# An RWKV attention stage rebuilt on 64-token chunks of two batch rows, ahead of a routed expert layer

## The chip, the cores and the metric

The kernel runs on one core of one Trainium2 chip, as one launch. The metric is the device time of that launch in microseconds. Its engines are TensorE (PE, with its weight loads shown apart as PEld), VectorE (DVE), ScalarE (ACT), GpSimd (POOL) and SyncE (SP, which here only issues DMAs). All tensors are fp32 except the one-hot matrices of the routing.

## The reference: what is computed

Two blocks stand one after the other. The first is a linear attention with a delta-rule state, for 4 batch rows, 8 heads, 768 tokens and a head dimension of 40:

```python
for t in range(S):
    y[:, :, t] = einsum('bhd,bhde->bhe', r_t, state)
    Sa = einsum('bhde,bhe->bhd', state, a_t)
    state = state * w_t[:, :, None, :] - einsum('bhd,bhe->bhde', Sa, b_t) + einsum('bhd,bhe->bhde', v_t, k_t)
```

The second takes the 3072 rows of 320 values that come out and runs a top-1 routed expert layer on them:

```python
logits = x @ w_gate                       # 8 experts
expert_idx = argmax(logits, axis=1)       # and the softmax weight of that expert: gate_w
y = relu(x_e @ w1[e]) @ w2[e]             # rows of expert e, F = 1024
out = gate_w[:, None] * y
```

## The kernel before

The token recurrence is turned into matrix products over chunks of 128 tokens of one batch row. A unit is one chunk of one row with all 8 heads; there are 24 units, and a batch row's six chunks follow one another through its state. Two heads lie above each other on the partitions (`rows(par)`, 40 of each 64), and four such pairs lie beside each other (`p`).

`prepare` (L154) forms the running product of the decays (four scans and a reciprocal on DVE), scales A, K and B by it, and turns V, K, B and the decay into token-major form by PE transposes. `systems` (L195) builds four products of 128x128 per head under a triangular mask: GT, NT, N and AT, from operands of 40 rows. Inside a chunk each token's update depends on the tokens before it, so a unit triangular system (1 - N) has to be solved. The kernel squares N five times (`product`, L187, once for N and once for its transpose, each a group of four 128x128 matmuls and an ACT copy out of PSUM) and `attend` (L219) applies the powers in turn to the right-hand side: eight steps of `apply` (L226), each four matmuls of 128x128 weights on 40 columns and one DVE addition (L252, L261), for each of the two halves. Then come the transposed solution (L265), the product ZT under its mask, the output (L279 to L293), the new state (L300, L306) and its transpose (L323). `route` (L328) computes the gate logits of the unit (L336, L340) and its softmax weight, scales the rows by it and stores them to a DRAM tensor `x_rows`.

The units are software-pipelined in the program text (`prepare` and `systems` of the next unit stand before `attend` of this one). The order on each engine is set by the framework's scheduler, which sorts the instructions by a modelled time; no order is written out by hand.

After the last unit the routing (L387 to L485) counts the tokens of each expert and builds gather and scatter indices, all on a few DVE instructions, two matmuls and one-hot products. Then eight experts follow in fixed groups of four tiles of 128 rows: an indirect gather from `x_rows` on the POOL queue, transposes, `layer1` (L514), `layer2` (L527), a copy out (L532) and an indirect scatter (L533). Expert weights come on SP's queue, the first two pairs after attention. A loop over overflow tiles ends the kernel (L562).

## Time and profile before

| what | value |
|---|---|
| median of 3 runs | 2147.67 us (2145.57 to 2150.49) |
| the profiled execution | 2146.03 us, of which the span from first to last instruction is 2144.2 us |
| PE busy | 2009.8 us, 12916 matmul records |
| DVE, ACT, POOL busy | 511.5, 417.3, 151.1 us |
| mean granted TensorE clock | 0.756 of full |
| DMA moved | 59.58 MB |

"Busy" is the time in which an engine had at least one instruction under way. PE's matmuls overlap, and a record's duration contains its way through the array: in a row such as "1.05 us x16" the spacing of the starts is what an instruction costs, not the mean duration. Each fp32 matmul appears as two records, each with its own weight load. The granted clock is 1.00 at 2.4 GHz and 0.50 at 1.2 GHz; a value between is a mean over a stretch that had both.

### The profile page before, as it was taken

To read this page: it belongs to the slowest core of one execution; us is meant where nothing else is said; L and a number is where in the kernel's file an instruction comes from. 1 tells how busy PE (TensorE), PEld (TensorE's weight loads), DVE (VectorE), ACT (ScalarE), POOL (GpSimd) and SP (SyncE) were. 2 spreads that over 40 slices of the span, in tenths; PEclk is the share of its full clock that TensorE was granted. 3 is DMA by queue.
4 is the path that set the end of the run, shared out by engine and by line. 5 is a ranking of instruction groups with operands and counts; after the bars stand their busy time and mean duration, and the time that the engine had idled before them with its cause. 6 is when DMAs were issued, how large, how long until landed. Compare 5 with 4: busy or idle time off the path is not lost.

```text
span 2144.2 us, 29192 instructions
## 1 busy us (share of the span) xinstructions
PE 2009.8 (94%) x12916; PEld 1751.6 (82%) x12916; DVE 511.5 (24%) x1157; ACT 417.3 (19%) x849; POOL 151.1 (7%) x185
## 2 busy tenths in 40 slices
PE   5999999999999999999999999999999876999998
PEld 5899999999998999999999989989898872544454
DVE  3313322232233222222321332232221114111110
ACT  1322122211221222122212212212222100000010
POOL 4000000000000000000000000000000003211011
PEclk9987668756766786678667657866777657999999
DMA  2000000000000000000000000000000005332210
GB/s 56 19 5 23 22 22 19 4 22 19 4 22 22 20 4 22 22 12 12 22 22 1 22 22 20 4 22 22 1 22 4 2 5 149 113 97 71 78 46 12
DMA packets 20560, 59.58 MB, mean 28 GB/s; under 512 B 2893, under 2 KB 14159, under 8 KB 18512
## 3 DMA queue, kind: packets, MB, share of 16 engines
q1 hardware_dynamic: 16992, 48.50, 7.9%
q0 software_dynamic: 3072, 9.18, 1.4%
q8 instruction: 102, 1.67, 0.3%
q14 instruction: 26, 0.21, 0.0%
q10 hardware_dynamic: 368, 0.01, 0.0%
HBM read 49.82 MB, written 9.18 MB: 28 GB/s over the span
## 4 chain that ended last, share of the span: by engine, by line
PE 75%; issue 13%; DVE 4%; POOL 2%; DMA 0%; ACT 0%; POOLq 0%; DVEq 0%; ACTq 0%
PE ps_q L228 20%; PE ps_NT L190 11%; PE ps_N L190 8%; PE ps_y L289 4%; PE ps_y L285 4%; PE ps_r L241 4%; PE ps_nat L169 4%; PE ps_r L235 3%; PE ps_y L279 2%; PE ps_ZT L179 2%; PE ps_GT L179 2%; PE ps_AT L179 1%; POOL out_dram L533 1%; PE ps_N L179 1%; DVE X L252 1%
## 5 line engine op out<-in xcount | busy, mean ns | idle before, releaser
L228 PE MATMUL ps_q<-X,NT 128*128 128x40 f32 x2304 | 352.8, 308 | 36.2 <-DVE X L252 36.2
L228 PEld LDWEIGHTS ps_q<-X,NT 128*128 128x128 f32 x2304 | 334.6, 223 | 48.2 <-DVE X L252 47.3
L190 PE MATMUL ps_NT<-NT,N 128*128 128x128 f32 x1920 | 286.5, 297 | 3.9 <-DVE N L183 2.7
L190 PEld LDWEIGHTS ps_NT<-NT,N 128*128 128x128 f32 x1920 | 244.6, 201 | 12.1 <-DVE N L183 5.1
L192 ACT COPY NT<-ps_NT 128x512 f32<-128x512 f32 x240 | 140.6, 586 | 424.9 <-PE ps_NT L190 424.9
L190 PE MATMUL ps_N<-N,NT 128*128 128x128 f32 x1536 | 212.1, 283 | 0.0
L190 PEld LDWEIGHTS ps_N<-N,NT 128*128 128x128 f32 x1536 | 197.2, 201 | 0.0
L514 PE MATMUL hp<-xgT,w 128*128 128x512 f32 (+1 forms) x384 | 191.4, 628 | 0.0
L252 DVE TENSOR_TENSOR X<-ps_q,X 128x160 f32<-128x160 f32 x240 | 77.9, 325 | 461.0 <-PE ps_q L228 461.0
L514 PEld LDWEIGHTS hp<-xgT,w 128*128 128x128 f32 (+1 forms) x384 | 63.2, 189 | 122.9 <-issue 121.7
L228 PE MATMUL ps_q<-Z,NT 128*128 128x40 f32 x768 | 140.1, 345 | 21.4 <-DVE Z L261 21.4
L228 PEld LDWEIGHTS ps_q<-Z,NT 128*128 128x128 f32 x768 | 132.2, 260 | 28.7 <-DVE Z L261 28.0
L527 PE MATMUL zp<-w,h_sb 128*128 128x320 f32 x512 | 145.0, 433 | 0.0
L192 ACT COPY N<-ps_N 128x512 f32<-128x512 f32 x192 | 112.5, 586 | 75.5 <-PE ps_N L190 75.5
L289 PE MATMUL ps_y<-natB,ZT 128*128 128x40 f32 x384 | 116.1, 415 | 9.4 <-DVE ZT L183 7.9
L527 PEld LDWEIGHTS zp<-w,h_sb 128*128 128x128 f32 x512 | 94.5, 191 | 34.5 <-issue 0.8
L285 PE MATMUL ps_y<-natK,AT 128*128 128x40 f32 x384 | 115.6, 414 | 0.0
L289 PEld LDWEIGHTS ps_y<-natB,ZT 128*128 128x128 f32 x384 | 100.9, 330 | 13.5 <-DVE ZT L183 13.5
L285 PEld LDWEIGHTS ps_y<-natK,AT 128*128 128x128 f32 x384 | 100.6, 329 | 1.6
L158 POOL MEMSET PT<- 128x4 f32 x24 | 2.5, 105 | 1322.8 <-PE ps_xT L336 1010.0
L169 PE MATMUL ps_nat<-ident,in 128*128 128x128 f32 x288 | 71.6, 417 | 24.7 <-DMA in<-in_packed_dram 16.7
L261 DVE TENSOR_TENSOR Z<-ps_q,X 128x160 f32<-128x160 f32 x96 | 31.2, 325 | 225.1 <-PE ps_q L228 225.1
(150 smaller groups left out, 1950.2 us busy)
## 6 DMA issues: line engine op xcount, KB each, us to landing
in<-in_packed_dram SPq DMA_DIRECT2D x48, 480.0 KB
w<-in_moe_w_dram SPq DMA_DIRECT2D x8, 1280.0 KB
w<-in_moe_w_dram SPq DMA_DIRECT2D x8, 1024.0 KB
x_rows<-xs SPq DMA_DIRECT2D x24, 160.0 KB
w<-in_moe_w_dram SPq DMA_DIRECT2D x8, 256.0 KB
xg<-x_rows,g_idx POOLq DMA_INDIRECT x32
out_dram<-zo,s_idx POOLq DMA_INDIRECT x32
wg_sb<-in_moe_w_gate_dram ACTq DMA_DIRECT2D x2, 4.0 KB
```

What stands on the lines that cost most here:

```text
L169: nc.tensor.transpose(ps[:, p, :], src[:, p, :], ident[:])
L179: nc.tensor.matmul(pss[par][:, p, :], lhsT=lhs(par, p), rhs=rhs(par, p), start=True, stop=True)
L190: nc.tensor.matmul(ps[:, p, :], lhsT=lhs[:, p, :], rhs=rhs[:, p, :], start=True, stop=True)
L192: nc.scalar.copy(t[:], ps[:])
L228: nc.tensor.matmul(q[:, p, :], lhsT=m[:, p, :], rhs=x[:, p, :], start=True, stop=True)
L235: nc.tensor.matmul(qs[par][:, p, :], lhsT=I[rows(par), A, p, :], rhs=ST[rows(par), p, :], start=(p == 0), stop=False, skip_group_check=True,)
L241: nc.tensor.matmul(qs[par][:, p, :], lhsT=d["GT"][par][:, p, :], rhs=nV[:, p, par, :D], start=(c == 0 and p == 0), stop=True, skip_group_c ...
L252: nc.vector.tensor_tensor(Xn[:], q[:], X[:], op=ALU.add)
L285: nc.tensor.matmul(qs[par][:, p, :], lhsT=d["AT"][par][:, p, :], rhs=nK[:, p, par, :D], start=(c == 0 and p == 0), stop=False, skip_group_ ...
L289: nc.tensor.matmul(qs[par][:, p, :], lhsT=ZT[par][:, p, :], rhs=nB[:, p, par, :D], start=False, stop=True, skip_group_check=True,)
L514: nc.tensor.matmul(hp[:, :cols], lhsT=g["w"][0][:dsz, db, fb * 128 : (fb + 1) * 128], rhs=g["xT"][:dsz, db, :cols], start=(db == 0), stop= ...
L527: nc.tensor.matmul(zp[:], lhsT=g["h"][:, fb, j * 128 : (j + 1) * 128], rhs=g["w"][1][:, fb, :], start=(fb == 0), stop=(fb == FB - 1),)
```

## The change

A unit is now 64 tokens of two batch rows: `(c, s)` with twelve chunks c and two pairs of rows s. Its sixteen (row, head) systems are `HD`, eight of them side by side (`g`) and two above each other (`par`). Every matmul of the attention works on a 64x64 tile of the array (40 or 64 rows, 64 or 40 columns), or on a 32x32 tile inside the inverse. `eh(par)` is one half of the partitions, `dh(par)` the other: products from `eh` to `eh` lie on the diagonal of the array, those from `eh` to `dh` or back off it. `turns` takes two lists of matmuls and issues two of each in turn.

The triangular system is no longer applied power by power. `invert` forms the inverse of each 64x64 system: both diagonal 32x32 blocks are inverted by four squarings (`inv_sq`) and products (`inv_tt`), with transposes on DVE, and the block below the diagonal is put together from them (`inv_w`, `inv_f`). `solve` then applies it in one product, once for the solution and once for its transpose. The two units of a pair go through each step one after the other.

`manual_schedule` fixes PE's order as the program writes it; the other engines stay with the scheduler. In one iteration PE works on the pair c (right-hand side, solution, state, output, logits) and on the products of the pair c + 1, with the inverse of c + 1 between the two `emit` calls. Loads for c + 2 are issued in iteration c, in pieces of 64 tokens. `emit` forms the token-major rows and their logits in one product with an identity beside the gate weights. The rows are stored unscaled; the softmax weights are computed once for all tokens at the beginning of the routing, written as an extra column of `x_rows`, and come back with the gathered rows, where `layer2` multiplies by them in the copy at L532. The functions not shown (`natural`, `zgram`, `turned`, `y_state`, `y_rest`) are lists of sixteen matmuls of the same kinds, `y_rest` of thirty-two, followed by one copy or one product with a mask.

```diff
--- before.py
+++ after.py
@@ -127,242 +121,488 @@
+        G = 2 * NP
+        T2 = 64
+        NS = S // T2
+        NB2 = B // 2
+        HD = [(g, par) for g in range(G) for par in range(2)]
+        def eh(par, n=D):
+            return slice(par * 64, par * 64 + n)
+        def dh(par, n=D):
+            return slice((1 - par) * 64, (1 - par) * 64 + n)
+        def qd(par, i):
+            q = 2 * (1 - par) + i
+            return slice(q * 32, q * 32 + 32)
+        kab_r = [[ring.tile([128, 2, 3, NP, T2], F32, name=f"kab{s}_{i}") for i in range(3)] for s in range(NB2)]
+        wp_r = [[ring.tile([128, G, T2 + 1], F32, name=f"wp{s}_{i}") for i in range(2)] for s in range(NB2)]
...
+                for lo in (32, 96):
+                    nc.gpsimd.memset(t[lo : lo + 32], 1.0)
+                nc.gpsimd.memset(t[:, :, 0:1], 0.0)
+        first = ring.tile([128, G, T2 + 1], F32, name="first")
+        nc.gpsimd.memset(first[:], 0.0)
+        nc.gpsimd.memset(first[:, :, 0:1], 1.0)
...
+        def turns(*lists):
+            lists = [list(l) for l in lists if l]
+            while any(lists):
+                for l in lists:
+                    for _ in range(2):
+                        if l:
+                            l.pop(0)()
...
+                for par in range(2):
+                    nc.sync.dma_start(
+                        d["wp"][eh(par), b2 * NP : b2 * NP + NP, 1:], packed[b, ch, par, :, W, :, o : o + T2],
+                    )
+                for par in range(2):
+                    nc.sync.dma_start(d["kab"][eh(par), b2], packed[b, ch, par, :, K : B_ + 1, :, o : o + T2])
...
+        def decay(u):
+            c, s = u
+            d = units[u]
+            PT = d["PT"] = sb.tile([128, G, T2 + 1], F32, name=f"PT{s}", bufs=3)
+            nc.vector.tensor_tensor_scan(
+                PT[:].rearrange("q g t -> q (g t)"), d["wp"][:].rearrange("q g t -> q (g t)"),
+                first[:].rearrange("q g t -> q (g t)"), 0.0, op0=ALU.mult, op1=ALU.add,
+            )
+            wi = sb.tile([128, 2, NP, T2], F32, name="wi")
+            P4 = PT[:].rearrange("q (b p) t -> q b p t", b=2)
+            for h in range(2):
+                nc.vector.reciprocal(wi[:, h], P4[:, h, :, 1:])
+            k = d["kab"]
+            for n, m in ((0, wi[:]), (1, P4[:, :, :, :T2]), (2, wi[:])):
+                nc.gpsimd.tensor_tensor(k[:, :, n], k[:, :, n], m, op=ALU.mult)
...
+            for g, par in HD:
+                if nm == "GT":
+                    l, r, h = kab(d, 0, g), kab(d, 1, g), eh(par)
+                else:
+                    l, r, h = vr(d, 0, g), vr(d, 1, g), dh(par)
+                ts.append(lambda l=l, r=r, h=h, g=g, par=par: mm(ps[eh(par, 64), g, :], l[h], r[h]))
+            def end():
+                t = d[nm] = sb.tile([128, G, T2], F32, name=f"{nm}{s}")
+                nc.scalar.copy(t[:], ps[:])
+                nc.gpsimd.tensor_tensor(t[:], t[:], up64[:, None, :].to_broadcast([128, G, T2]), op=ALU.mult)
+            return ts, end
...
+        def quads(f):
+            for g in range(G):
+                for i in range(2):
+                    for par in range(2):
+                        f(g, par, i)
...
+            def one(g, par, i):
+                a, b = kab(d, 1, g), kab(d, 2, g)
+                h = eh(par)
+                if i == 0:
+                    mm(ps[qd(par, 0), g, 32:], a[h, :32], b[h, :32])
+                else:
+                    mm(ps[qd(par, 1), g, :], a[h, 32:], b[h, :])
+            quads(one)
+            N = d["N"] = sb.tile([128, G, 32], F32, name=f"N{s}", bufs=3)
...
+            quads(lambda g, par, i: mm(ps[qd(par, i), g, :], NT[qd(par, i), g, :], N[qd(par, i), g, :]))
+            N = d["N"] = sb.tile([128, G, 32], F32, name=f"N{s}", bufs=3)
+            nc.scalar.copy(N[:], ps[:])
+            if k < 3:
+                NT = d["NT"] = sb.tile([128, G, 32], F32, name=f"NT{s}", bufs=3)
+                nc.vector.transpose(NT[:].rearrange("q g t -> q (g t)"), N[:].rearrange("q g t -> q (g t)"))
...
+            quads(lambda g, par, i: mm(ps[qd(par, i), g, :], N[qd(par, i), g, :], TT[qd(par, i), g, :]))
+            TTn = d["TT"] = sb.tile([128, G, 32], F32, name=f"TT{s}", bufs=3)
+            nc.vector.tensor_tensor(TTn[:], ps[:], TT[:], op=ALU.add)
...
+            def one(g, par, i):
+                h = qd(par, 1)
+                mm(ps[qd(par, i), g, :], (n21[h, g, :], i32[h, :])[i], TT[h, g, :])
+            quads(one)
+            nc.scalar.copy(x_r[s][:, :, 32:], ps[:])
...
+            def one(g, par, i):
+                h = qd(par, i)
+                mm(ps[h, g, :], (t11[h, g, :], i32[h, :])[i], X[h, g, :])
+            quads(one)
...
+        def invert(us):
+            for u in us:
+                inv_n(u)
+            for k in range(4):
+                for u in us:
+                    inv_sq(u, k)
+                for u in us:
+                    inv_tt(u)
+            for u in us:
+                inv_w(u)
+            for u in us:
+                inv_f(u)
+        st = {}
...
+            ps = bank("ps_q", D)
+            ts = []
+            if c:
+                ST = st[s][0]
+                for g, par in HD:
+                    ts.append(lambda g=g, par=par: mm(
+                        ps[dh(par, 64), g, :], kab(d, 1, g)[eh(par)], ST[eh(par), g, :D],
+                        start=(g == 0), stop=False, free=True))
+            for g, par in HD:
+                ts.append(lambda g=g, par=par: mm(
+                    ps[dh(par, 64), g, :], d["GT"][eh(par, 64), g, :], d["nV"][eh(par, 64), g, :],
+                    start=(c == 0), free=True))
...
+            q, F = d["q"], d["F"]
+            t1 = [lambda g=g, par=par: mm(p1[eh(par, 64), g, :], F[dh(par, 64), g, :], q[dh(par, 64), g, :D])
+                  for g, par in HD]
+            t2 = [lambda g=g, par=par: mm(p2[dh(par, 64), g, :], q[dh(par, 64), g, :], F[dh(par, 64), g, :])
+                  for g, par in HD]
...
+            ts = []
+            for n, (l, r) in enumerate((("nK", "nV"), ("nB", "u"))):
+                for g, par in HD:
+                    ts.append(lambda n=n, l=l, r=r, g=g, par=par: mm(
+                        ps[eh(par, (64, D)[n]), g, :], d[l][eh(par, 64), g, :], d[r][eh(par, 64), g, :],
+                        start=(n == 0 and g == 0), stop=(n == 1), free=True))
...
+                        mm(pv[b2 * 64 : b2 * 64 + 64, par, p, :], d["y"][eh(par), b2 * NP + p, :], iw[eh(par), p, :])
...
+        with tc.manual_schedule(engines={mybir.EngineType.PE}):
+            pairs = [[(c, s) for s in range(NB2)] for c in range(NS)]
+            for u in pairs[0] + pairs[1]:
+                load_kab(u)
...
+            invert(pairs[0])
+            for c in range(NS):
+                us = pairs[c]
+                nx = pairs[c + 1] if c + 1 < NS else [None] * NB2
+                if c + 2 < NS:
+                    for u in pairs[c + 2]:
+                        load_kab(u)
+                for u, n in zip(us, nx):
+                    q, qe = right(u)
+                    k, ke, b, be = [], None, [], None
+                    if n:
+                        k, ke = natural(n, "K")
+                        b, be = natural(n, "B")
+                    turns(q, k + b)
+                    qe()
+                    if n:
+                        ke(), be()
+                for u, n in zip(us, nx):
+                    y = y_state(u)
+                    if n:
+                        g, ge = gram(n, "GT")
+                        turns(y, g)
+                        ge()
                     else:
+                        turns(y)
+                    t1, e1, t2, e2 = solve(u)
+                    turns(t1, t2)
+                    e1(), e2()
+                for u in us:
+                    (z, ze), (t, te) = zgram(u), state(u)
+                    turns(z, t)
+                    ze(), te()
+                if c + 2 < NS:
+                    for u in pairs[c + 2]:
+                        decay(u)
+                for u, n in zip(us, nx):
+                    tt, tte = turned(u)
+                    y, ye = y_rest(u)
+                    a, ae, v, ve = [], None, [], None
+                    if n:
+                        a, ae = gram(n, "AT")
+                        v, ve = natural(n, "V")
+                    turns(y, tt + a + v)
+                    ye(), tte()
+                    if n:
+                        ae(), ve()
+                if c + 2 < NS:
+                    for u in pairs[c + 2]:
+                        load_vr(u)
+                emit(us[0])
+                if nx[0]:
+                    invert(nx)
+                emit(us[1])
@@ -382,6 +622,21 @@
+        nc.vector.tensor_reduce(lmin[:], lgn[:], axis=AX, op=ALU.min)
+        gex = sm_pool.tile([128, NT, E], F32)
+        nc.vector.tensor_tensor(gex[:], lmin[:].unsqueeze(2).to_broadcast([128, NT, E]), lgn[:], op=ALU.subtract)
+        nc.scalar.activation(gex[:], gex[:], AF.Exp)
+        gs = sm_pool.tile([128, NT], F32)
+        nc.vector.reduce_sum(gs[:], gex[:], axis=AX)
+        nc.vector.tensor_scalar_add(gs[:], gs[:], 1e-9)
+        nc.vector.reciprocal(gs[:], gs[:])
+        xw = x_d[:, Dm : Dm + 1].rearrange("(s b c t) o -> b s t (c o)", b=2, t=64, s=B // 2)
+        for b2 in range(2):
+            for s in range(B // 2):
+                nc.scalar.dma_start(
+                    xw[b2, s], gs[b2 * 64 : b2 * 64 + 64, s * (S // 64) : (s + 1) * (S // 64)],
+                )
@@ -529,7 +784,7 @@
-            nc.scalar.copy(zo[:], zp[:])
+            nc.scalar.activation(zo[:], zp[:], AF.Copy, scale=g["xg"][:, j, Dm:])
```

## Rows read from the trace of the kernel before

**Rows 1.** The page: span, busy time by engine, engines on the final chain.

```profile
span 2144.2 us, 29192 instructions
...
PE 2009.8 (94%) x12916; PEld 1751.6 (82%) x12916; DVE 511.5 (24%) x1157; ACT 417.3 (19%) x849; POOL 151.1 (7%) x185
...
PE 75%; issue 13%; DVE 4%; POOL 2%; DMA 0%; ACT 0%; POOLq 0%; DVEq 0%; ACTq 0%
```

**Rows 2.** Busy time in four stretches, then granted clock, DMA share, GB/s.

```profile
0.00:45.00 45.00, 19.96 (x120) 18.73 (x120) 16.07 (x22) 4.80 (x8) 26.75 (x51) 1.00 0.25 66
45.00:1768.71 1723.71, 1644.33 (x11776) 1564.01 (x11776) 434.46 (x963) 379.71 (x778) 57.04 (x66) 0.71 0.06 15
1768.71:1786.70 17.99, 2.66 (x28) 2.44 (x28) 15.05 (x43) 0.00 (x0) 4.90 (x4) 0.50 0.91 292
1786.70:2144.20 357.50, 342.88 (x992) 166.43 (x992) 45.90 (x130) 32.76 (x64) 62.37 (x64) 0.97 0.23 70
```

**Rows 3.** PE groups by shape: busy us, mean ns, idle before and its releaser.

```profile
L228 PE MATMUL ps_q<-X,NT 128*128 128x40 f32 x2304 | 352.8, 308 | 36.2 <-DVE X L252 36.2
L190 PE MATMUL ps_NT<-NT,N 128*128 128x128 f32 x1920 | 286.5, 297 | 3.9 <-DVE N L183 2.7 <-ACT N L192 0.7
...
L323 PE MATMUL ps_st<-ident,ST 40*40 40x40 f32 x320 | 28.2, 264 | 0.4 <-ACT S L325 0.4
...
L300 PE MATMUL ps_s<-natV,natK 128*40 128x40 f32 x320 | 15.0, 267 | 0.0
```

**Rows 4.** PE alone in three stretches: busy (records), granted clock, DMA share, GB/s.

```profile
1124.00:1131.00 7.00, 7.00 (x65) 0.50 0.06 23
1060.00:1083.00 23.00, 23.00 (x203) 1.00 0.01 1
69.40:72.90 3.50, 3.50 (x58) 1.00 0.02 5
```

**Rows 5.** Timeline of PE, small tiles: start us, us, line, tiles, count.

```profile
175.05 1.05 PE L323 MATMUL ps_st<-ident,ST 40*40 40x40 f32 x16
...
1098.11 0.76 PE L300 MATMUL ps_s<-natV,natK 128*40 128x40 f32 x16
...
1107.91 0.75 PE L323 MATMUL ps_st<-ident,ST 40*40 40x40 f32 x8
```

**Rows 6.** Timeline of PE, the same two-column products near 96 us.

```profile
96.20 0.51 PE L300 MATMUL ps_s<-natV,natK 128*40 128x40 f32 x16
96.53 0.41 PE L306 MATMUL ps_s<-u,natB 128*40 128x40 f32 x12
```

**Rows 7.** Groups of DVE, ACT and POOL by shape, columns as in Rows 3.

```profile
L161 DVE RECIPROCAL in<-PT 128x512 f32<-128x512 f32 x24 | 80.5, 3353 | 0.8
...
L160 DVE TENSOR_TENSOR_SCAN PT<-in,zeros_c 128x128 f32<-128x128 f32 x96 | 33.4, 406 | 18.0 <-DMA in<-in_packed_dram 15.6 <-POOL PT L158 1.0
...
L183 DVE TENSOR_TENSOR ZT<-ps_ZT,before 128x512 f32<-128x512 f32 x48 | 30.9, 686 | 149.9 <-PE ps_ZT L179 149.8
...
L192 ACT COPY N<-ps_N 128x512 f32<-128x512 f32 x192 | 112.5, 586 | 75.5 <-PE ps_N L190 75.5
...
L532 ACT COPY zo<-zp 128x320 f32<-128x320 f32 x32 | 13.7, 427 | 134.3 <-PE zp L527 134.3
...
L163 POOL TENSOR_TENSOR in<-in 128x512 f32<-128x512 f32 x24 | 31.3, 1306 | 49.5 <-DVE in L161 49.5
...
L134 POOL MEMSET in<- 32x2560 f32 x6 | 13.3, 2224 | 0.3
```

**Rows 8.** DMA: one queue of the page, and the loads of the attention.

```profile
q1 hardware_dynamic: 16992, 48.50, 7.9%
...
in<-in_packed_dram SPq DMA_DIRECT2D x48, 480.0 KB
```

**Rows 9.** Timeline of POOL at the start.

```profile
23.18 1.35 POOL L162 TENSOR_TENSOR in<-in,PT 128x512 f32<-128x512 f32 x1
```

**Rows 10.** Timeline of POOL at the end of the routing.

```profile
1786.70 1.18 POOL L495 DMA_INDIRECT xg<-x_rows,g_idx  x1 [2.18 <-DVE ta L482]
```

More of the change, by code (lines that the diff above doesn't have):

```diff
@@ L174, in product2 @@
-        def product2(lhs, rhs, mask, tag, bufs):
-            pss = [big("ps_" + tag) for _ in range(2)]
-            for p in range(NP):
-                for par in range(2):
-                    nc.tensor.matmul(pss[par][:, p, :], lhsT=lhs(par, p), rhs=rhs(par, p), start=True, stop=True)
-            ts = []
-            for par in range(2):
-                t = sb.tile([128, NP, 128], F32, name=tag, bufs=bufs)
-                nc.vector.tensor_tensor(t[:], pss[par][:], mask[:, None, :].to_broadcast([128, NP, 128]), op=ALU.mult)
-                ts.append(t)
-            return ts
@@ new lines, in eh @@
+        def eh(par, n=D):
[7 more added lines that the diff above has]
+        wp_r = [[ring.tile([128, G, T2 + 1], F32, name=f"wp{s}_{i}") for i in range(2)] for s in range(NB2)]
+        x_r = [ring.tile([128, G, 64], F32, name=f"xt{s}") for s in range(NB2)]
@@ new lines @@
+        for q in range(4):
+            qs = slice(q * 32, q * 32 + 32)
+            nc.gpsimd.tensor_copy(i32[qs], ident[qs, qs])
+            nc.gpsimd.tensor_scalar(low32[qs], after[qs, qs], scalar1=-1.0, scalar2=None, op0=ALU.mult)
+        up64 = ring.tile([128, T2], F32, name="up64")
+        for q in range(2):
+            qs = slice(q * 64, q * 64 + 64)
+            nc.gpsimd.tensor_copy(up64[qs], before[qs, qs])
+        for t in x_r:
+            nc.gpsimd.memset(t[:], 0.0)
+            for q in (0, 2):
+                qs = slice(q * 32, q * 32 + 32)
+                nc.gpsimd.tensor_copy(t[qs, :, 0:32], i32[qs, None, :].to_broadcast([32, G, 32]))
@@ new lines, in load_vr, with kab, vr @@
+        def load_vr(u):
+            c, s = u
+            d = units[u]
+            d["vr"] = sb.tile([128, 2, 2, NP, T2], F32, name=f"vr{s}")
+            for b2 in range(2):
+                ch, o, b = src(u, b2)
+                for par in range(2):
+                    nc.sync.dma_start(d["vr"][dh(par), b2], packed[b, ch, par, :, V : R + 1, :, o : o + T2])
+        def kab(d, n, g):
+            return d["kab"][:, g // NP, n, g % NP, :]
+        def vr(d, n, g):
+            return d["vr"][:, g // NP, n, g % NP, :]
@@ new lines, in solve, with end1, end2 @@
+        def solve(u):
+            c, s = u
+            d = units[u]
+            p1, p2 = bank("ps_u", D), bank("ps_uT")
+            q, F = d["q"], d["F"]
[3 more added lines that the diff above has]
+                  for g, par in HD]
+            def end1():
+                t = d["u"] = sb.tile([128, G, D], F32, name="u")
+                nc.scalar.copy(t[:], p1[:])
+            def end2():
+                t = d["uT"] = sb.tile([128, G, T2], F32, name="uT")
+                nc.scalar.copy(t[:], p2[:])
+            return t1, end1, t2, end2
@@ new lines, in turned, with end @@
+        def turned(u):
+            c, s = u
+            if c + 1 == NS:
+                return [], lambda: None
+            ps = bank("ps_S", D)
+            ts = [lambda g=g, par=par: mm(ps[dh(par, 64), g, :], st[s][0][eh(par), g, :], ident[eh(par), par * 64 : par * 64 + D])
+                  for g, par in HD]
+            def end():
+                Sn = s_r[s][c % 2]
+                nc.scalar.copy(Sn[:, :, :D], ps[:])
+                st[s] = (st[s][0], Sn)
+            return ts, end
@@ new lines, in y_state @@
+        def y_state(u):
+            c, s = u
+            d = units[u]
+            if s == 0:
+                wide["y"] = pp.tile([128, 2, G, T2], F32, name="ps_y", tag="wide", bufs=1)
+            ps = d["py"] = wide["y"][:, s]
+            if not c:
+                return []
+            Sn = st[s][1]
+            return [lambda g=g, par=par: mm(
+                ps[eh(par, 64), g, :], Sn[dh(par), g, :], vr(d, 1, g)[dh(par)], start=(g == 0), stop=False, free=True)
+                for g, par in HD]
@@ new lines, in y_rest, with end @@
+        def y_rest(u):
+            c, s = u
+            d = units[u]
+            ps = d["py"]
+            ts = []
+            for n, (l, r) in enumerate((("nK", "AT"), ("nB", "ZT"))):
+                for g, par in HD:
+                    ts.append(lambda n=n, l=l, r=r, g=g, par=par: mm(
+                        ps[eh(par, (64, D)[n]), g, :], d[l][eh(par, 64), g, :], d[r][eh(par, 64), g, :],
+                        start=(c == 0 and n == 0 and g == 0), stop=(n == 1), free=True))
+            def end():
+                t = d["y"] = sb.tile([128, G, T2], F32, name="y")
+                nc.vector.tensor_tensor(t[:], ps[:], d["PT"][:, :, :T2], op=ALU.mult)
+            return ts, end
```

374 lines of the change are left out of this document (165 added, 209 removed).

## The prediction

> **What bounds the kernel now.** I read the page first [rows 1]: PE is busy for 94% of a span of 2144.2 us and carries 75% of the chain of waits, so the work in front of the last instruction is PE's. The profiled execution took 2146.03 us, 1.8 us more than its span; the median of the runs shown is 2147.67 us, 1.6 us above it, so a sum made against the profile needs no correction of size. The stretches [rows 2] split it: 45.0 us of start, 1723.7 us of attention, 18.0 us of routing, 357.5 us of expert layers. The reader should see there that DVE is busy for 434 and ACT for 380 of the 1724 us, and that the granted clock is 0.71: in attention PE moves between its two levels, 1.2 and 2.4 GHz.
>
> What PE does in those 1724 us is in the grouped instructions [rows 3]. Each fp32 matmul stands as two records (L190: 24 units x 2 halves x 5 levels x 4 matmuls = 960, and 1920 records). At full clock 203 records fill 23.0 us [rows 4], 113 ns each, whether 128 or 40 columns move: the 128-column weight load is as long as a 128-column matmul. Attention issues about 480 records per unit and 24 units, 72 us a unit. That is the price the change attacks.
>
> **What a small tile costs.** Three shapes of before answer to the new ones, all at half clock [rows 5]. Eight 40x40 records in one tile take 0.75 us of which the last record's own 0.26 is the tail: 67 to 70 ns each, start to start. Sixteen in two tiles on the array's diagonal (rows and columns 0-63 beside 64-127) take 1.05 us, 53 each although they overlap only in part. Sixteen 128x40 records in two column tiles take 0.76 us with a tail of 0.27: 33 each, half of one tile's price. At full clock sixteen such records start within 0.33 us, 20 ns each, with twelve more behind them [rows 6]. So a tile takes time in proportion to its columns, and tiles run side by side. A tile of 64 columns is 67 x 64/40 = 107 ns at half clock; with two tiles in turn 53, with four 27. No row has four tiles: the bounds are 27 (all overlap) and 53 (two at a time); I take 27, since two were shown to overlap fully. A 32x32 tile is 53 ns, 13 with four in turn. Nothing in the trace shows so short a spacing for long: no longer run is closer than 60 ns (58 records in 3.5 us, [rows 4]), so the price of issuing a record is open between 13 and 60. The nearest rows are 20 and 33; I take 25, between them.
>
> **Which clock.** The four product stages GT to AT work K=40 row tiles in pairs, 65 records in 7.0 us without a gap, and stay at 0.50; the level is 1.00 in the 128x128 products [rows 4]. The change has no 128x128 product left, so I take half clock for all of attention. Full clock is a rival.
>
> **The sum.** Records per unit (two batch rows, 64 tokens; again 24 units), from the diff. 64-column matmuls: natural K, V, B 48; GT and AT 32; right 32; solve 32; zgram 16; state 32; turned 16; y_state 16; y_rest 32; emit 16: 272, or 544 records. In turns() and in emit 480 of them have four tiles to go round, 64 (the longer list's rest in z/state and in y_rest) two: 480 x 27 + 64 x 53 = 13.0 + 3.4 = 16.4 us. The inverse: 32 matmuls each in inv_n, four times sq and tt, w, f: 352, or 704 records x 25 = 17.6 us. A unit is 34.0 us against 72, a pair 68.
>
> Waits of a pair: in a round of the inverse PE has four blocks of 64 records, 1.6 us each. After one block ACT copies 256 columns (427 ns for 320 and 586 for 512 give 0.38, [rows 7]), DVE transposes them (no row; bounds 0.2 and 0.7 around half of the 686 for 512 columns, taken 0.42), each with some 0.2 of latency: 1.2 us, and three other blocks (4.8 us) cover it. What is bare: emit of the first unit waits for the y product of the second (0.69 us on DVE behind PE's drain), and the tile shape changes four times; I take 2 us. A pair then takes 70.
>
> Other engines per pair [rows 7]: DVE two scans of 520 columns (4 x 406 each), four reciprocals of 256 (3353 for 512), four masks and y of 0.69, twenty short ones of 0.42, some more: 24 us. ACT: 16 us by 586 for 512 and 427 for 320 columns. POOL: ten products of 512 columns at 1.31 and two short: 14 us. None is near 70. The next chunk's decays (9.9 us of DVE in one piece) stand ahead of the y product in the program, but PE has y_rest, AT and V meanwhile, 320 records or 10 us. If that cover goes (faster PE) some 4 us a pair come bare; that is in the rival at full clock.
>
> Transfers: the loads become 92,160 runs of 256 bytes (3,840 a unit), where 48 loads of 480 KB moved before [rows 8]. By bytes against the mean packet (2.85 KB, 7.9% x 16 x 2144 / 16992 = 0.159 us) a run costs 14 ns on one of 16 engines, 82 us in all; at most it costs as much as that packet, 916 us in all, 76 us a pair, which would just bind. I take the lower: hidden, as the loads are issued a full iteration ahead; without that cover it costs 6 us a pair, 66 in all. On SP's queue the stores of emit wait for its copy, and the loads of the next iteration stand behind them, but those are not due before the iteration after.
>
> Start: before, POOL's first product began at 23.18 [rows 9], behind POOL's memsets. The new ones: 12 of 32x1536 (1.33 each by the 2.22 for 2560), 8 of 32x520, 14 pads and the small constants, 30 us in all with 4 us of unchanged ones before them. The first natural K comes at about 38; naturals and GT, AT of two units 320 x 27 = 8.6; their inverse, with nothing beside it, 35; edges 5: the loop starts at 87.
>
> Loop: 11 x 70 = 770. The last chunk has 288 records a unit and nothing to fill its waits: 17 + 9 = 26. End of attention at 883. Routing 18.0 and experts 357.5 stay [rows 2]: exp and sums on whole tiles add 1.5 us on DVE beside it, the scale rides on an ACT copy that waits for PE. The first gather (at 1786.70, [rows 10]) now also waits for 3,072 four-byte writes of the weights, issued on ACT's queue some 3 us into routing, where ACT has nothing behind them but the first layer's copies: between nothing and 3072 x 0.159 / 16 = 30 us after issue, so 0 to 17 late, while weight loads fill the queues (DMA share 0.91 there, [rows 2]); I take 5. Sum: 87 + 770 + 26 + 18.0 + 357.5 + 5 + 1.8 = **1265 us**.
>
> **Rivals.** *Full clock.* If the clock stays up over the small tiles as it does over the 128x128 products, 64-column records cost 15 and 29 ns, the inverse's 20 [rows 6]: 7.2 + 1.9 + 14.1 = 23.2 a unit, 46 a pair, and 8 of waits since DVE's decays come bare: 54. Start 72, last chunk 20: 72 + 594 + 20 + 382 = 1068. For it: dense PE; against it: GT to AT [rows 4].
>
> *A price per record.* If each record costs about 50 ns however small, a unit's 1,248 records take 62.4, a pair 127, start 129, last chunk 38: 129 + 1397 + 38 + 382 = 1946. For it: no long run closer than 60; against it: 20 and 33 ns [rows 5, 6], though those runs of 16 and 28 records are shorter than any stage of the inverse. By the Trainium skill (TensorEngine Tiling (Array Packing), Instruction Overhead) a matmul has some 60 cycles of overhead; as an estimate 50 ns at 1.2 GHz, and paid one after the other it would give this rival's time. The two-tile rows at 33 disagree with paying it in series.
>
> *Tiles of one list block each other, and the kernel is slower.* Every list here writes one bank from different row tiles; the diagonal pair of [rows 5] wrote two banks, and the 128x40 pair, which shares a bank, has no row tiles. If row tiles take turns at a bank, four tiles run as two (two lists, two banks) at 53, two as one at 107, and the inverse, one bank at a time, at 53 to 107: 25.4 + 6.8 + 42.4 = 74.6 a unit, 151 a pair; 145 + 1661 + 42 + 382 = 2230. It decides from a mean of 57 ns per record, where the new sum passes the old time: 2146 less 382 behind attention and 74 of start and waits, over 29,760 records (mine is 27). The Trainium skill (same page, Gotcha 1: PSUM Pressure) says that different row tiles cannot access the same bank at once; no run here shows it so far.
>
> That the change does not do what it says is no case: the records are counted from its text.
>
> **How the numbers follow.** The forecast at half clock, its small covers gone or not, has 0.56 (1150 to 1480: 20 to 33 ns per inverse record is -84 to +135, the DMA and gather bounds +66 and +12); full clock 0.27 (1000 to 1150); price per record 0.10 (1600 to 2100); blocked tiles 0.07 (some of it under 57 ns a record). The range leaves out the two last and the fastest edge: 1000 to 1600. Faster by over 0.2% (about what measurement can tell here) 0.93, within it 0.01, slower 0.06.
>
> **What would show it.** If I am right: some 29,600 matmul records in attention; GT, solve and y_rest records 25 to 30 ns apart on average, sq and tt about 25, granted clock near 0.5 up to the expert layers; one chunk pair every 70 us; PE's idle time before emit and inv_n near 2 us a pair; first gather under 25 us after the last logits. The clock at 1.0 would show the first rival; equal spacing near 50 in all shapes the second; par 0 and par 1 of one list never closer than a tile's time the third. A pair that waits for loads, or DVE in front of PE's transposes, would prove my covers wrong.

## The result, and the profile after

The changed kernel takes 1320.11 us (median of 4 runs, 1317.20 to 1321.18) against 2147.55 us of the kernel before (4 runs, 2145.57 to 2150.49): 0.614 of the time, 95% interval 0.613 to 0.616. The forecast was 1265 us, with 1000 to 1600 as its range. Direction and range held; the kernel is 55 us longer than the sum said, nearly all of it in the attention, and the reason is not one that the prediction names.

The page of the kernel after, against [rows 1]:

```profile
span 1318.3 us, 64132 instructions
PE 947.3 (72%) x30652; PEld 735.6 (56%) x30652; DVE 337.6 (26%) x627; ACT 222.8 (17%) x496; POOL 286.3 (22%) x302
...
q8 instruction: 241, 3.95, 1.3%
...
issue 43%; PE 39%; POOL 9%; DVE 5%; DMA 1%; SPq 1%; ACT 0%; POOLq 0%; ACTq 0%; DVEq 0%
```

PE is no longer busy all the time, and no other engine has taken its place: the chain of waits gives 43% to "issue", time in which PE waited for nothing that the profile shows. The line to notice is q8, which carries PE's program: 241 packets of 16 KB. PE executes 2 x 30652 = 61304 instructions (each record of a matmul is a weight load and a matmul), and 61304 / 241 is 254 (255.6 with the 287 semaphore instructions of its trace): one packet is 256 instructions of 64 bytes, or nearly 128 records.

Busy time in four stretches, roughly start, loop, last chunk, and routing with experts, against [rows 2]; after each span PE and PEld, DVE, ACT, POOL, then granted clock, DMA share, GB/s. The cut at 87 us is the forecast's. The loop's own first product starts at 94.31 us and the last chunk's at 914.02. The trace has no record of the clock before 95.9 us, so the 1.00 of the first row is no reading.

```profile
0.00:87.00 87.00, 30.03 (x1493) 28.58 (x1494) 29.95 (x35) 10.28 (x23) 59.04 (x109) 1.00 0.30 66
87.00:900.00 813.00, 542.70 (x27152) 510.68 (x27151) 240.18 (x402) 170.06 (x395) 159.15 (x125) 0.63 0.14 31
900.00:935.00 35.00, 27.56 (x955) 26.50 (x955) 4.88 (x11) 5.25 (x12) 0.00 (x0) 0.64 0.04 8
935.00:1318.00 383.00, 346.97 (x1052) 169.79 (x1052) 62.62 (x181) 37.20 (x67) 68.13 (x68) 0.95 0.26 80
```

The records of attention are 1493 + 27152 + 955 = 29600, as forecast. The second stretch has 27152 of them in 813 us: 29.9 ns each, with PE busy for two thirds of it. What PE waited for (total us, times, longest):

```profile
PE ps_tt L208 <- issue: 84.4, 47, 2.3
PE ps_sq L208 <- issue: 73.3, 41, 2.3
PE ps_nat L208 <- POOL kab L257: 41.8, 1, 41.8
PE ps_w L208 <- issue: 22.1, 12, 2.4
```

Nearly every such wait is close to 2 us. Where they stand is seen in PE's timeline in the middle of one inverse (start, length, records, and the idle time before):

```profile
503.58 1.91 PE L208 MATMUL ps_sq<-N,NT 32*32 32x32 f32 x125 [1.61 <-DVE NT L323]
507.43 0.32 PE L208 MATMUL ps_sq<-N,NT 32*32 32x32 f32 x3 [1.94 <-issue]
507.56 1.92 PE L208 MATMUL ps_tt<-TT,N 32*32 32x32 f32 x124
511.42 0.32 PE L208 MATMUL ps_tt<-TT,N 32*32 32x32 f32 x4 [1.94 <-issue]
511.55 1.88 PE L208 MATMUL ps_sq<-N,NT 32*32 32x32 f32 x123
515.12 0.32 PE L208 MATMUL ps_sq<-N,NT 32*32 32x32 f32 x5 [1.69 <-issue]
```

The stop is in the middle of a list, after 3 + 124 or 4 + 123 records, 127 every time: not a dependence of the program, but the end of a packet. PE runs through a packet in 1.9 us (some 14 ns a record) and then stands for 1.9 us. Each stop ends at a nearly fixed distance from a packet of q8. As medians over the 143 stops of more than 1 us in this stretch: 1.19 us after PE resumed, a packet begins; it takes 1.10 us; 1.40 us after its end PE resumes. That is a round trip of 3.7 us, or 3.9 by the means (1.31, 1.12 and 1.43). The stretch has 213 packets, 3.82 us apart on average; 213 round trips are 790 to 820 us of its 813: it is as long as the arrival of its instructions.

By stages of one pair (PE alone: right; z and state; y_rest; the levels of the inverse) the same rate shows beside very different clocks. The columns are the stretch's length, PE's busy time, records, granted clock, DMA share and GB/s:

```profile
466.09:473.69 7.60, 7.24 (x266) 0.50 0.49 114
479.74:486.72 6.98, 3.52 (x209) 1.00 0.27 62
486.72:497.29 10.57, 7.68 (x330) 0.84 0.19 42
503.58:534.34 30.76, 15.94 (x1028) 0.50 0.07 16
```

That is 29, 33, 32 and 30 ns per record, for 64x64 tiles and for 32x32, at half clock and at full. The first row shows a limit to this reading: PE is busy for 7.24 of the 7.60 us, so at half clock the 64x64 records themselves cost nearly what arrival allows. In the loop such records start 27.9 ns apart between stops at half clock and 17.4 at full; the stops of over 0.3 us take 10% of the time in the one case and 40% in the other. In the attention of the kernel before, no 128 records in a row took less than 11.0 us; its packets came 18.5 us apart (median), never under 10.8, longer than the round trip here.

### The profile page after: what moved, and what is told of

It is laid out like the page before. It is cut to its first block, busy times and chain, and to the rows that moved or that the text cites. A ratio compares the mean times of both kernels' runs of the same rounds, so it can differ in the third digit from the quotient of the medians.

```text
span 1318.3 us, 64132 instructions
## 1 busy us (share of the span) xinstructions
PE 947.3 (72%) x30652; PEld 735.6 (56%) x30652; DVE 337.6 (26%) x627; ACT 222.8 (17%) x496; POOL 286.3 (22%) x302
## 3 DMA queue, kind: packets, MB, share of 16 engines
q1 hardware_dynamic: 110356, 48.52, 14.3%
## 4 chain that ended last, share of the span: by engine, by line
issue 43%; PE 39%; POOL 9%; DVE 5%; DMA 1%; SPq 1%; ACT 0%; POOLq 0%; ACTq 0%; DVEq 0%
PE ps_tt L208 7%; PE ps_sq L208 7%; PE ps_nat L208 4%; PE ps_f L208 3%; PE ps_y L208 3%; PE ps_q L208 3%; DVE wi L254 3%; POOL out_dram L788 2%; PE ps_s L208 2%; POOL xg L750 2%; PE ps_w L208 2%; PE ps_u L208 1%; POOL kab L257 1%; PE ps_GT L208 1%; DVE PT L247 1%
## 5 line engine op out<-in xcount | busy, mean ns | idle before, releaser
L208 PE MATMUL ps_tt<-TT,N 32*32 32x32 f32 x6144 | 105.8, 236 | 88.5 <-issue 84.4
L208 PE MATMUL ps_sq<-N,NT 32*32 32x32 f32 x6144 | 104.6, 236 | 87.9 <-issue 73.3
L208 PEld LDWEIGHTS ps_tt<-TT,N 32*32 32x32 f32 x6144 | 94.9, 151 | 95.3 <-issue 90.7
L208 PEld LDWEIGHTS ps_sq<-N,NT 32*32 32x32 f32 x6144 | 94.5, 151 | 95.6 <-issue 95.5
L208 PE MATMUL ps_nat<-ident,kab 40*64 40x40 f32 x1536 | 85.1, 295 | 44.8 <-POOL kab L257 41.8
L208 PEld LDWEIGHTS ps_nat<-ident,kab 40*64 40x64 f32 x1536 | 81.4, 212 | 46.6 <-POOL kab L257 41.8
L254 DVE RECIPROCAL wi<-PT 128x256 f32<-128x256 f32 x48 | 82.1, 1733 | 5.3 <-POOL kab L257 3.9
L257 POOL TENSOR_TENSOR kab<-kab,wi 128x512 f32<-128x512 f32 x48 | 65.7, 1381 | 33.3 <-DVE wi L254 33.3
L296 POOL TENSOR_TENSOR AT<-AT,up 128x512 f32<-128x512 f32 x24 | 41.9, 1747 | 108.5 <-ACT AT L295 108.5
L208 PE MATMUL ps_f<-xt,i 32*32 32x64 f32 x768 | 45.5, 305 | 7.4 <-issue 7.4
```

The lines of the kernel that those rows point to most:

```text
L208: nc.tensor.matmul(out_, lhsT=lhs, rhs=rhs, start=start, stop=stop, skip_group_check=free)
L254: nc.vector.reciprocal(wi[:, h], P4[:, h, :, 1:])
L257: nc.gpsimd.tensor_tensor(k[:, :, n], k[:, :, n], m, op=ALU.mult)
L296: nc.gpsimd.tensor_tensor(t[:], t[:], up64[:, None, :].to_broadcast([128, G, T2]), op=ALU.mult)
```

## Experiments

Theory A: PE's instructions arrive at one packet of 256 per round trip of about 3.9 us, 30 ns per fp32 record whatever its shape. Theory B: 30 ns is the price of the tiles themselves. Theory C: row tiles block each other at a PSUM bank. The code lines below are abridged; a time without a range is a single run.

**The price by itself.**

```
stream("p32four", 32, 32, four)        # size, columns, tiles; 320 matmuls each
stream("p32half", 32, 16, four)
stream("p32one", 32, 32, four[:1])
stream("p64four", 64, 64, [(0, 0, 0), (1, 1, 0), (0, 1, 1), (1, 0, 1)], 2)
stream("p64diag", 64, 64, [(0, 0, 0), (1, 1, 0)])          # one bank
stream("p64diag2b", 64, 64, [(0, 0, 0), (1, 1, 1)], 2)     # two banks
stream("p64one", ...), stream("p128", ...), stream("p32again", ...)
```

> The whole computation is left out: nine streams of 320 matmuls (640 records, 5 packets of 16 KB at 256 instructions each) run one after the other on PE, each in one shape. Theory A (PE's instructions arrive at one 16 KB packet per round trip of 3.9 us): every small shape settles at about 30 ns per record in bursts of 127 or 128 records with a gap of near 2 us between them: 32x32 with 32 columns in four tiles 30, with 16 columns 30, 64x64 with 64 columns in four tiles 30; only a shape whose tile time is longer shows it (64x64 in one tile 107 at half clock or 53 at full, diagonal pair 53 or 30, 128x128 57 or more). Theory B (30 ns is the tiles' own price): the streams go without gaps, 32 columns in four tiles about 30, 16 columns about 15, 64x64 in four tiles about 30. Theory C (row tiles block each other at one PSUM bank): the diagonal pair of 64x64 tiles in one bank takes twice what it takes in two banks.

The first stream on PE's timeline, and then all nine stretches in the order of the list (length, PE busy, records, clock, DMA share, GB/s):

```profile
4.75 3.21 PE L86 MATMUL p32four<-x 32*32 32x32 f32 x223 [4.75 <-DMA x<-in_moe_w_dram]
9.90 1.93 PE L86 MATMUL p32four<-x 32*32 32x32 f32 x128 [1.95 <-issue]
14.17 1.93 PE L86 MATMUL p32four<-x 32*32 32x32 f32 x128 [2.35 <-issue]
18.45 1.93 PE L86 MATMUL p32four<-x 32*32 32x32 f32 x128 [2.35 <-issue]
22.45 0.65 PE L86 MATMUL p32four<-x 32*32 32x32 f32 x33 [2.07 <-issue]
```

```profile
4.75:22.87 18.12, 9.40 (x640) 1.00 0.59 206
25.04:44.08 19.04, 10.07 (x639) 1.00 0.01 3
46.23:80.33 34.10, 34.10 (x640) 1.00 0.01 2
81.88:98.54 16.66, 11.95 (x639) 1.00 0.02 4
103.16:125.07 21.91, 21.74 (x640) 0.85 0.01 3
127.20:146.50 19.30, 18.98 (x640) 1.00 0.02 4
148.53:215.09 66.56, 66.56 (x639) 0.52 0.01 1
216.72:290.79 74.07, 74.07 (x639) 0.96 0.00 1
292.39:308.42 16.03, 7.86 (x640) 0.65 0.02 4
```

Behind its first records no stream waits for another engine, and yet 223 records run, and then PE stands for 2 us after each 128. Half the columns are no faster (19.04 against 18.12 us): A, not B. The first 223 records without a stop show why the short runs of [rows 5, 6] told nothing of this: PE begins with nearly two packets at hand. Where a tile costs more than arrival, the stops vanish: one 32x32 tile 53.4 ns a record, one 64x64 tile 106.7 at half clock. (The trace has no record of the clock before 85.7 us; the 1.00 of the first three rows is no reading.) The diagonal pair in one bank goes at about 53 ns up to 109 us, at half clock, which is half the price of one tile, and at 29.1 without a stop once the clock has risen; in two banks it is 29.1 too. C is out for this pair: two row tiles that write different partitions of one bank do not slow each other. The Trainium skill says that different row tiles cannot access one bank at the same time (TensorEngine Tiling (Array Packing), Gotcha 1: PSUM Pressure); for this pair these rows disagree.

**Half the columns in the kernel.**

```
- mm(ps[qd(par, i), g, :], NT[qd(par, i), g, :], N[qd(par, i), g, :])
+ mm(ps[qd(par, i), g, :16], NT[qd(par, i), g, :], N[qd(par, i), g, :16])      # tt alike
```

> Every sq and tt product moves 16 of its 32 columns (the other half of each product is left out and filled with a copy of the first); the number of PE instructions is the same. Theory A (instruction arrival): 1310 to 1335 us, PE's records in sq and tt still about 30 ns apart with gaps of 2 us. Theory B (the tiles' own price): 1024 records per pair at 15 in place of 30 ns, 15 us a pair, 12 pairs: about 1140 us.

1320.5 us. The groups of the inverse, which stood at 105.8 and 104.6 us busy with 84.4 and 73.3 of issue:

```profile
L208 PE MATMUL ps_tt<-TT,N 32*32 32x16 f32 x6144 | 103.0, 210 | 90.5 <-issue 85.9 <-POOL TT L329 2.3 <-POOL kab L257 2.2
L208 PE MATMUL ps_sq<-N,NT 32*32 32x16 f32 x6144 | 102.5, 209 | 88.0 <-issue 73.1 <-DVE NT L323 12.6 <-DVE NT L342 1.9
```

Half of the moved columns of 1024 records a pair is worth nothing.

**The same columns in fewer instructions.**

```
  # per level: [N_next | N*T] in one product
+ mm(ps[q, g, lo:hi], NT[q, g, :], NX[q, g, lo:hi])      # NX = [N | T], 5 lists
- mm(ps[q, g, :], NT[q, g, :], N[q, g, :])               # sq, 4 lists
- mm(ps[q, g, :], N[q, g, :], TT[q, g, :])               # tt, 4 lists
```

> The square of one level and the product of the level before share their weights and become one matmul of 64 columns: 5 lists of 32 matmuls in place of 8, the same number of moved columns, 384 records (3 packets of 256 instructions) fewer per pair. Theory A (instruction arrival): 3 x 3.9 = 11.7 us less a pair, 12 pairs, 140 us: 1180 us, up to 1220 if the shorter rounds no longer cover the copies and transposes between levels. Theory B (time goes by columns): 1320 us, within 15.

1179.8 us, to the microsecond what A said.

```profile
span 1178.0 us, 54857 instructions
...
PE 911.2 (77%) x26044; PEld 696.7 (59%) x26044; DVE 337.4 (29%) x651; ACT 222.3 (19%) x496; POOL 294.2 (25%) x326
...
q8 instruction: 205, 3.36, 1.2%
```

36 packets fewer, 140.3 us less: 3.9 us a packet. They still come 3.81 us apart, so arrival binds this kernel too.

**The packets beside other traffic.**

```
+ for i in range(6):
+     nc.scalar.dma_start(extra_d[c, i], moe_w1[i])      # each chunk, 1.28 MB each
```

> In every chunk ACT's queue also copies six blocks of 1.28 MB from DRAM to DRAM, which nothing reads. PE's work and order are the same. Theory A (instruction arrival): the 16 KB instruction packets take longer than 1.1 us beside this traffic, the gaps of PE grow by as much in the same stretches, and the time grows by 3% to 30% (1360 to 1700 us). Theory B (the tiles' own price, or a fixed price per instruction): PE's gaps stay near 1.9 us and the time stays within 15 us of 1320, unless PE is seen to wait for loads.

1441.6 us. The waits answer to those above:

```profile
PE ps_sq L208 <- issue: 102.4, 42, 4.2
PE ps_tt L208 <- issue: 90.7, 47, 3.6
...
PE ps_sq L208 <- DVE NT L341: 18.2, 1, 18.2
```

The time went as A says, but the packets did not take longer (1.09 us on average, 1.12 before). They began later after PE resumed: 1.74 in place of 1.31 us on average, though the median moved only from 1.19 to 1.30, so a part of the packets was held up much longer. They came 4.28 us apart, and the loop takes 914 in place of 820 us: 94 of the 121 us. The rest is in the start: the loop begins at 120.3 in place of 94.3 us, and 18.2 us of that is the last line above: ACT began its copy of a square only after 21.4 idle us, which the trace puts down to a load of kab, and its queue issues the extra copies. So this run is no clean test of arrival alone.

**Undoing parts of the change.** The turns:

```
- for l in lists: take two of each in turn
+ for l in lists: all of l, then the next
```

> Undoes the turns: the lists of 64x64 products go one after the other, so that two tiles in place of four alternate; PE's instructions are the same in number and kind. Theory A (instruction arrival at 30 ns per record): two 64-column tiles in turn cost 29 ns per record at full clock and 53 at half (the diagonal pair of the streams), so only stretches at half clock can pass the arrival rate: 480 records of a unit by at most 23 ns, 24 units: 1320 to 1585 us, and 1320 to 1400 if these stretches go to full clock as z and state do. Theory B (30 ns is the price of four tiles that share the array): two tiles cost twice that, 60 ns, 480 x 30 ns x 24 = 345 us more: about 1665 us.

1358.4 us: inside A's range, far from B's 1665. Two tiles in turn mostly keep up with arrival. The hand order:

```
- with tc.manual_schedule(engines={mybir.EngineType.PE}):
+ if True:
```

> Undoes the order of PE written by hand (the scheduler puts PE's instructions as it does those of the other engines); the instructions themselves are the same. Theory A: no order can go under the arrival of 240 packets, so not below 1310 us; above it by the waits that this order leaves bare on PE between dependent stages, some 1.5 us per level of the inverse if the two units no longer cover each other: up to 10 x 1.5 x 12 = 180 us, 1320 to 1500. The rival, that the hand order itself made the time: 1500 us or more.

1305.6 us, one run, 15 below the changed kernel and 4 below the floor that I gave: its 213 packets came 3.76 us apart. The hand order is not what made the time.

**Further down.** w and f without their products with the identity:

```
- quads(one)                       # (n21, i32) x TT, (t11, i32) x X
+ mm(ps[qd(par, 0), g, :], n21[h, g, :], TT[h, g, :])      # the i = 0 half alone
+ nc.gpsimd.tensor_copy(Ft[qd(par, 1), :, 32:], TT[qd(par, 1)])
```

> e2_merged, and the w and f stages of the inverse without their products with the identity (POOL and ACT copy these blocks): 128 records fewer per pair than e2_merged, 512 fewer than the changed kernel. Theory A (instruction arrival): one packet of 256 instructions, 3.8 us, less per pair than e2_merged's 1180, 12 pairs: 1134 us. The rival, that two blocks of 64-column records no longer cover copy and transpose (1.5 us a level) or that the array binds at half clock: 1150 to 1180 us, PE waiting for DVE and ACT in place of issue.

1146.3 us, between what A and its rival said; 193 packets: 12 fewer for 33.5 us, 2.8 each. A pair takes 59.8 us, 15.5 packets of 3.86. Of the 12 us that are missing against A some 6 are waits inside the inverse: PE's waits there for DVE, ACT and POOL are 37 us in all, against 31 in the merged kernel. The other half was not followed. Then transposes for half of the turns through the identity, and another start:

```
- mm(out_, x, ident)                                       # two records
+ nc.tensor.transpose(out_, x, ident) if at0 else mm(out_, x, ident)
```

> e7_merged_trimmed, with half of the turns through the identity (those whose result lies in partitions 0 to 63) as transposes, one record in place of two (32 records of a unit, half a packet a pair), and with most start-up memsets on DVE in place of POOL. Theory A: 12 x 1.9 = 23 us less by the records, and the first natural K at about 27 in place of 41.8 us, 15 us: e7's time less 38, about 1096 us. If the array or the waits have become the bound, less by the start alone: 15.

1372.7 us, 277 above what I expected, though the start came (first natural K at 28.0). In PE's timeline the L215 lines are transposes:

```profile
199.53 0.22 PE L215 MATMUL ps_nat<-ident,vr 40*64 40x40 f32 x1
199.68 0.30 PE L211 MATMUL ps_nat<-ident,vr 40*64 40x40 f32 x2
199.92 0.22 PE L215 MATMUL ps_nat<-ident,vr 40*64 40x40 f32 x1
200.07 0.31 PE L211 MATMUL ps_nat<-ident,vr 40*64 40x40 f32 x2
```

A start every 0.15 to 0.24 us (x2 is one matmul with its two records). Whether each transpose costs this, or each change between the kinds, was measured by itself:

```
side = n // run % 2
if turned and side == 0: nc.tensor.transpose(o, x[h, ...], ident[h, h])
else:                    nc.tensor.matmul(o, lhsT=x[h, ...], rhs=ident[h, h], ...)
stream("m2", 2, False); stream("t2", 2, True); stream("t8", 8, True); stream("t24", 24, True); stream("m24", 24, False)
```

> The whole computation is left out: five streams of 240 turns through the identity, 64x64, in runs that alternate between two tiles on the diagonal and two banks. m2 and m24 use matmuls alone (2 records each), in runs of 2 and 24; t2, t8 and t24 use a transpose (one record) in every other run, of 2, 8 and 24. e9_start's trace shows a record start about 155 ns after the one before it wherever a transpose stands beside a matmul. Theory D (the array drains at each change between the two kinds, not at each transpose): t2 has 120 changes, 18 us and more beside its records; t8 30, 5 us; t24 10, 1.5 us, so t24 is shorter than m24 by its quarter fewer records. Theory E (each transpose drains by itself): t2, t8 and t24 all cost some 120 x 155 ns = 19 us or more beside their matmuls.

The stretches t2, t8, t24 and m24, all at half clock:

```profile
23.65:80.54 56.89, 56.89 (x360) 0.51 0.00 1
82.17:125.13 42.96, 42.96 (x359) 0.50 0.00 1
126.76:166.52 39.76, 39.76 (x359) 0.50 0.01 1
168.15:216.00 47.85, 47.85 (x479) 0.50 0.01 1
```

D: t2 has 110 changes more than t24 and is 17.1 us longer, 0.156 us a change; t24 is 8 us shorter than m24. This is the price against t24, whose long runs in one tile do not overlap; what alternating between two tiles gains without transposes (m2 put 447 records into 15.8 us) is lost besides. A pair of e9_start has 64 transposes, so some 128 changes: 20 us, and its pair is 20.2 us longer than that of e7_merged_trimmed.

Without transposes, with inv_n as one 64x64 product and the new start:

```
- mm(ps[qd(par, 0), g, 32:], a[h, :32], b[h, :32]); mm(ps[qd(par, 1), g, :], a[h, 32:], b[h, :])
+ mm(ps[dh(par, 64), g, :], kab(d, 1, g)[h], kab(d, 2, g)[h])
+ most kab, wp memsets: nc.gpsimd -> nc.vector; load_vr(pairs[0]) ahead of load_kab(pairs[1])
```

> e7_merged_trimmed (1146 us), with inv_n as one 64x64 product per head (32 records of a unit fewer, half a packet a pair; the mask and the first transpose on DVE become 0.5 us longer), most start-up memsets on DVE and the first vr loads ahead of the second chunk's. No transposes. Theory A (instruction arrival): 12 x 1.9 = 23 us less by the records, 6 more by DVE's longer first step, 14 less by the first natural K at about 28 in place of 42.5 us: 1115 us. The rival, that the array or the waits between levels bind by now: 1130 us, the start alone.

and the same with the hand order taken out as above:

> e10_fewer without the hand-written order of PE. If the scheduler's order hides the waits as it did for the changed kernel (1305.6 against 1320): 1100 us. The rival, that with shorter blocks its order leaves the levels of the inverse bare: 1130 to 1200 us.

1137.2 us (1135.5 to 1140.6) and, with the scheduler's order, 1128.5 us (1123.3 to 1129.6): 0.526 of the kernel before, interval 0.524 to 0.528, and the fastest of all. Both lie near their rivals' 1130, not A's 1115 and 1100. With the hand order the first natural K came 14.4 us earlier, but the loop only 7.2 (75.0 against 82.2), as the second unit's kab and the levels of the first inverse were waited for. The half packet a pair gave next to nothing: 187 packets, a pair at 59.7 against 59.9, and PE now waits for DVE's first transpose:

```profile
PE ps_sq L216 <- issue: 40.7, 44, 2.1
...
PE ps_sq L216 <- DVE NT L326: 27.4, 10, 4.3
```

Here the waits of the inverse have begun to bind beside arrival, as the rival had it. A last try, back at the old inv_n and the hand order, turned K and B by one matmul of 128 weight columns:

```
+ mm(pss[par][:, g, :], d["kab"][eh(par), b2, p, 0:2, :], ident[...])      # [K | B], 64x128 tile
- mm(ps[eh(par, 64), g, :], x[h], ident[h, at : at + D])                   # K and B, 64x64 each
```

> e10_fewer (hand order of PE, the new start), but inv_n as in e7_merged_trimmed, and K and B turned by one matmul of 128 weight columns per head in place of two of 64 (32 records of a unit, half a packet a pair; two short copies more on ACT per unit, and three loads of kab per batch row and parity in place of one). Theory A (instruction arrival): e7's 59.8 us a pair less 1.9, start 14 earlier: 1146 - 14 - 12 x 1.9 = 1109 us. The rival, that the waits between the levels of the inverse take back what the records give, as in e10_fewer: 1125 to 1140 us.

1266.7 us (1265.7 to 1272.8): both theories wrong. A pair takes 70.8 us. Where 64x128 tiles alternate with the 64x64 tiles of right, eight records take 0.94 us, where arrival alone would make it 0.24:

```profile
439.67 0.44 PE L211 MATMUL ps_q<-ST,kab 40*64 40x40 f32 x4
440.03 0.65 PE L211 MATMUL ps_kb<-ident,kab 40*128 40x40 f32 x4
440.61 0.44 PE L211 MATMUL ps_q<-ST,kab 40*64 40x40 f32 x4
440.98 0.65 PE L211 MATMUL ps_kb<-ident,kab 40*128 40x40 f32 x4
```

Some 0.35 us per change; 32 changes a pair make 11 us, and the pair is 11 us longer than that of e7_merged_trimmed. That it is the change of the tile's size, and not something else about these two lists, was not tried by itself.

## Why the prediction was right in direction and 55 us short

- **The cost of a record** is the step that failed. The sum had 16.4 us a unit for 64-column matmuls and 17.6 for the inverse at 25 ns, taken between rows of 20 and 33, and 2 us of waits a pair: 70. Measured: 30.0 ns a record, 74.5 us a pair. PE alone, from the loop's first product to the last chunk and in the last chunk:

```profile
94.31:914.02 819.71, 545.68 (x27329) 0.63 0.13 31
914.02:936.93 22.91, 19.92 (x584) 0.75 0.05 12
```

The inverse was undersized (704 x 30.0 = 21.1, so 7.0 us a pair more), and the 2 us of waits do not come on top, since the stops for packets cover them. The loop is 50 us longer than its 770. The first inverse, 1408 records with nothing beside them, took 42.1 us and not 35. The last chunk took 3 us less than its 26.
- **The 64-column term** came near (544 x 30.0 = 16.3), rightly at half clock, where four tiles do overlap at 27.9 ns against the forecast's 27, and by luck at full clock, where their own 17 ns are stretched to 29 by the stops. That the total lies in the range is luck in the same sense: 30.0 is inside the 20 to 33 taken for the inverse, but those bounds were the price of issuing a record and not of its arrival.
- **Why**: the prediction asked what a tile and what the issue of one record cost, and read both from runs of 16 and 28 records. These rows hold: within a packet the 32x32 records do go at 13 to 14 ns. What was missing is that instructions come from memory. At [rows 4]'s pace a packet lasts longer than the 3.9 us of its round trip (128 x 60 ns = 7.7 us); at 14 ns it does not (1.8 us). The rule that bears on it is in the Trainium skill (Runtime: NRT & Kernel Launch, Instruction fetch mechanics): code comes in blocks of 16 KiB, 256 instructions, and crossing into the next is mostly hidden. The size agrees with q8 here; that it is hidden does not, at 1.9 us in each 3.9.
- **Half clock for all of attention** was wrong as a fact (0.63 in the loop, 1.00 in z and state) and cost nearly nothing, since at either level a record comes out near 30 ns. For the same reason the full-clock rival's 1068 us was out of reach: below 30 ns per record no clock helps.
- **The rival of 50 ns per record** had the right form, a price that ignores shape, at the wrong size. The blocked tiles fell in the streams; that rival's 42.4 us for the inverse is 60 ns a record, for which it gives no reason between its 53 and 107.
- **Covers**: loads and DVE's decays stayed hidden, as argued; of PE's waits for other engines in the loop the largest is DVE NT L323, 14.3 us in 9 times. ACT's copy and DVE's transpose took 0.37 and 0.44 us, for 0.38 and 0.42. No row gave the 0.2 us of latency at each of them; between engines the trace shows some 0.03. By its own 82 us, bare loads would have cost 6.8 and not 6 us a pair, and the terms of its half-clock range reach down to 1181, not 1150; neither decides anything here.
- **Start**: the first natural K came at 41.8, not 38, behind POOL's kab products; with the first inverse 7 us longer, and less for edges than the 5 allowed, the loop began at 94.3 for 87.
- **Tail**: routing and experts took 381.4 us from DVE's first operation, against 375.5 [rows 2]. The first gather comes 22.8 us after that operation and waited 6.15 us for the writes of the weights, where I had taken 5.

## What to carry to other kernels

When tiles get small, count instructions as well as columns: divide PE's instructions by 256, multiply by the round trip of a packet (3.7 to 3.9 us here), and compare with the time that the tiles' own prices give; the longer of the two is the stage. The sign in a trace is a stop of PE on "issue" in the middle of a list, every 128 fp32 matmul records. The cure is fewer instructions for the same columns (shared weights, no products with an identity), until the waits between dependent steps bind instead, as they began to at 187 packets. Transposes and matmuls should not alternate in one order; for sizes of tile one trace suggests the same.

## What the runs showed of the hardware that was not expected

- PE's instructions arrive at 256 per 3.8 us (3.76 to 3.82 on average in the changed kernel, e1_half_columns, e2_merged and e4_no_hand_order); with 94 MB of other copies beside them, 4.28.
- PE starts from rest with 223 records at hand, nearly two packets (e6_streams).
- A change between fp32 transposes and matmuls on PE costs 0.156 us at half clock (e12_turn_streams); alternation made a kernel with fewer instructions 226 us slower than its parent.
- Two diagonal 64x64 tiles that write one PSUM bank in different partitions are as fast as in two banks, 29 ns a record at full clock, and at half clock take half the time of one tile (53 against 106.7 ns).
